# A new decoding of the float64 weights, a new first score step and a new order of issue in an attention and spatial-gate kernel

## The chip, the cores and the metric

The kernel runs on one core of a Trainium2 chip. The metric is the device time of one execution in microseconds (us), from the first to the last instruction of the core with what lies around them; the median of several runs is compared. TensorE (PE) multiplies, VectorE (DVE), ScalarE (ACT) and GpSimd (POOL) work on elements, SyncE (SP) only issues transfers (DMA). Every engine works off its own queue in order and waits at an instruction whose inputs are not there.

## What is computed

Two steps: attention against 32 memory slots for each of 8 batches and 8 heads, and a gated feed-forward over all heads together, whose gate mixes the 576 tokens by a spatial matrix.

```python
def _attn_ref(q, k, v, phi):                 # q, k, v: 8, 8, 576, 64; phi: 8, 8, 576, 32
    a = np.exp(phi - np.max(phi, axis=2, keepdims=True))
    a = a / (np.sum(a, axis=2, keepdims=True) + 1e-09)
    k_m = np.einsum('bhsm,bhsd->bhmd', a, k)
    v_m = np.einsum('bhsm,bhsd->bhmd', a, v)
    scores = np.matmul(q, k_m.transpose(0, 1, 3, 2)) / np.sqrt(q.shape[-1])
    scores = scores - np.max(scores, axis=-1, keepdims=True)
    attn = np.exp(scores)
    attn = attn / (np.sum(attn, axis=-1, keepdims=True) + 1e-09)
    return np.matmul(attn, v_m)

def _moe_ref(x, w_in, w_spatial, b_spatial, w_out):   # x: 8, 576, 512, heads side by side
    h = np.maximum(x @ w_in, 0.0)            # w_in: 512, 1024
    u, v = (h[..., :512], h[..., 512:])
    v_n = (v - mean(v)) / np.sqrt(var(v) + 1e-06)
    v_s = np.einsum('ts,bsd->btd', w_spatial, v_n) + b_spatial[None, :, None]
    return (u * v_s) @ w_out                 # w_out: 512, 512
```

`w_in` and `w_out` arrive as float64. The kernel reads each number as two 32-bit words and makes an fp32 number of them on chip; this is called decoding below.

## The kernel before

The work is cut into steps with one letter each; a function is a generator, and every `yield` ends one step. For each batch b:

- P (`memory_weights`): loads `phi` (single buffer `phi_sb`), takes the maximum over tokens, exponentiates, sums (`es`). The maximum and the sum run over 9 rows of a partition by `over_rows`, in four operations each.
- K (`memories`): loads `k` and `v` (single buffer `kv_sb`), multiplies them by the exponentials (`kvm`, 144 matmuls as the trace counts them), divides by the sums, transposes to `kT` and `vT`.
- Q (`queries`): loads `q` and transposes it to `qT`, for b = 0 on TensorE from one plain load, for b > 0 on VectorE from four loads whose packets are 128 bytes.
- S (`scores`): `sc` = memory slots on partitions, tokens along the row; four VectorE transposes to `sm`, softmax there, transposes back, then the split into a rounded part `ah` and its remainder `al`.
- M0, M1 (`products`): `mp` = `vT` times the decoded `win_sb`, the u half (0) or the v half (1); split into `mh` and `ml`.
- V0 to V4 (`gate`): `pv` = attention times M's v half, for 128 tokens (V4 for 64); relu, mean and variance on VectorE, the inverse root in three small POOL operations, the normalisation on ScalarE, then the split into `vh` and `vl`, `t1` and `t2` for V4.
- U0 to U3 (`units`): `pu`, the u half, relu. G0 to G3 (`spatial`): `ps` = the normalised gate times the transposed spatial matrix `wth`, `wtl`, 28 matmuls; product with `u`; split into `gh`, `gl`. O0 to O4 (`project`): `po`, 12 matmuls, and the store.

Once for the program: D loads `w_in`, L and E decode its u and v half in two blocks of 1024 numbers a partition each, X loads and decodes `w_out` in four blocks of 512, W loads the spatial matrix, T0 to T4 (`transpose_spatial`) transpose it.

Which engine an edit of a step takes is decided by the set `ON_VECTOR`: a remainder (`low`) that is not in it is made on TensorE by one matmul with `minus` and copied out by ScalarE; decoding operations that are not in it go to POOL or ScalarE.

The order is written out by hand. `START` lists the steps of batch 0 with the weight steps, and first steps of batches 1 and 2 (one prime ahead of a batch each); `PLAN` is walked for b = 1 to 7. Inside `manual_schedule` each engine gets its instructions in the order in which the steps issue them. PSUM has four single banks (`bank`) and two double ones (`banks`); a step that finds none free makes TensorE wait for the engine that empties one.

## Time and profile before

| | us |
|---|---|
| median of 3 runs | 422.83 |
| lowest and highest run | 422.32, 423.84 |
| span of the profiled execution | 421.1 |

| engine | busy us | share of the span |
|---|---|---|
| PE | 392.9 | 93% |
| DVE | 295.7 | 70% |
| ACT | 237.0 | 56% |
| POOL | 76.7 | 18% |

The profiled execution is one run; its span ends with the last instruction, and 1.7 us lie between it and the median. A busy PE is one that has a matmul in it, not one at its peak; the matmuls are pipelined, so what counts is the distance between two starts. In the chain that ended last, PE has 83% of the span. The page's 40 slices show PE below nine tenths in the first five (2, 1, 8, 7, 7 tenths of 10.5 us each) and in the last. The DMA engines are busy at nine tenths in the first slices and at about half later.

### The profile page before, as it was taken

The numbers are of one execution on the slowest core, as the hardware profiler recorded it, in microseconds if no ns is written. First come the engines' busy times: TensorE is split into PE (matmuls) and PEld (weight loads), VectorE is DVE, ScalarE is ACT, GpSimd is POOL, SyncE is SP. The second block draws the span as 40 slices with busy tenths as digits, with TensorE's granted clock in tenths as the row PEclk, the third lists the DMA queues.
The fourth block names the chain that finished last, engine by engine and source line by source line (L and its number), as shares of the span: only waits on it lengthen the run. The fifth ranks groups of instructions, "written<-read, shape, count | busy, mean of one in ns | idle before, by whom it ended". The sixth has DMA issues, their size and how long they took to land.

```text
span 421.1 us, 9279 instructions
## 1 busy us (share of the span) xinstructions
PE 392.9 (93%) x3828; PEld 331.0 (79%) x3828; DVE 295.7 (70%) x560; ACT 237.0 (56%) x446; POOL 76.7 (18%) x154
## 2 busy tenths in 40 slices
PE   2187799999999999999999999999999999999995
PEld 1072687979888897979798898879797888889884
DVE  2889998994997568945896569946996568834420
ACT  2948888666743575447735575346735576248321
POOL 1336046522200121022200120002100120013000
PEclk9999999999999999999999999999999999999998
DMA  8999947118922748084905467064905400020003
GB/s 291 399 379 277 199 143 156 12 50 165 196 86 55 128 170 170 2 131 134 227 7 71 111 195 146 1 132 141 198 27 75 107 2 2 2 100 2 0 26 100
DMA packets 85790, 50.69 MB, mean 120 GB/s; under 512 B 66226, under 2 KB 70322, under 8 KB 85748
## 3 DMA queue, kind: packets, MB, share of 16 engines
q1 hardware_dynamic: 85748, 50.10, 47.7%
q8 instruction: 30, 0.49, 0.5%
q14 instruction: 12, 0.10, 0.1%
HBM read 40.65 MB, written 9.44 MB: 119 GB/s over the span
## 4 chain that ended last, share of the span: by engine, by line
PE 83%; DVE 7%; ACT 3%; DMA 3%; issue 2%; POOL 1%; POOLq 0%; SPq 0%; DVEq 0%; ACTq 0%
PE ps L701 28%; PE po L741 23%; PE pu L663 11%; PE pv L597 9%; PE kvm L375 4%; PE mp L565 3%; PE sc L492 2%; DMA w_sb<-in_moe_w_spatial_dram 2%; DMA out_dram<-o 1%; ACT raw L208 1%; PE pv L607 1%; PE pv L606 1%; PE wt L287 1%; DVE phi_sb L349 1%; DVE win_sb L223 1%
## 5 line engine op out<-in xcount | busy, mean ns | idle before, releaser
L701 PE MATMUL ps<-wth,vh 128*128 128x288 f32 x256 | 57.0, 304 | 0.3 <-ACT vh L639 0.3
L723 ACT CAST gh<-g 128x512 fp32r<-128x512 f32 x32 | 19.8, 620 | 63.8 <-DVE g L712 63.6
L701 PE MATMUL ps<-wth,vl 128*128 128x288 f32 x256 | 54.9, 296 | 0.0
L701 PE MATMUL ps<-wtl,vh 128*128 128x288 f32 x256 | 54.5, 294 | 0.0
L626 POOL TENSOR_SCALAR rs<-mv 128x1 f32<-128x1 f32 (+1 forms) x40 | 9.1, 227 | 248.3 <-DVE mv L623 247.9
L741 PE MATMUL po<-woh,gl 128*128 128x512 f32 x128 | 50.8, 397 | 0.0
L741 PE MATMUL po<-woh,gh 128*128 128x512 f32 x128 | 50.5, 395 | 0.0
L701 PEld LDWEIGHTS ps<-wth,vh 128*128 128x128 f32 x256 | 41.1, 188 | 11.5 <-ACT mh L574 5.0
L741 PE MATMUL po<-wol,gh 128*128 128x512 f32 x128 | 50.1, 391 | 0.0
L747 ACT COPY o<-po 128x512 f32<-128x512 f32 x36 | 21.1, 587 | 45.4 <-PE po L741 29.0
L701 PEld LDWEIGHTS ps<-wth,vl 128*128 128x128 f32 x256 | 41.1, 188 | 0.3 <-DVE vl L641 0.3
L701 PEld LDWEIGHTS ps<-wtl,vh 128*128 128x128 f32 x256 | 41.0, 188 | 0.0
L636 ACT ACTIVATE vr<-vr,sh,rs 128x512 f32<-128x512 f32 (+1 forms) x40 | 32.5, 814 | 9.3 <-POOL sh L631 9.0
L621 DVE BATCH_NORM_STATS2 st<-vr 128x6 f32<-128x512 f32 (+1 forms) x40 | 27.5, 687 | 14.0 <-ACT vr L602 13.8
L712 DVE TENSOR_TENSOR g<-u,ps 128x576 f32<-128x576 f32 x32 | 23.4, 751 | 12.5 <-PE ps L701 12.5
L741 PEld LDWEIGHTS po<-woh,gl 128*128 128x128 f32 x128 | 24.0, 188 | 7.5 <-DVE gl L725 2.1
L663 PE MATMUL pu<-ah,mh 128*128 128x288 f32 x128 | 28.8, 306 | 0.4 <-ACT u L672 0.4
L544 DVE TENSOR_TENSOR al<-aT,ah 128x576 fp32r<-128x576 f32 x16 | 12.1, 754 | 23.6 <-ACT ah L542 23.6
L741 PEld LDWEIGHTS po<-wol,gh 128*128 128x128 f32 x128 | 24.1, 188 | 4.6
L741 PEld LDWEIGHTS po<-woh,gh 128*128 128x128 f32 x128 | 24.0, 188 | 4.7
L663 PE MATMUL pu<-al,mh 128*128 128x288 f32 x128 | 27.4, 295 | 0.0
L663 PE MATMUL pu<-ah,ml 128*128 128x288 f32 x128 | 27.3, 294 | 0.0
(158 smaller groups left out, 887.3 us busy)
## 6 DMA issues: line engine op xcount, KB each, us to landing
kv_sb<-in_k_dram SPq DMA_DIRECT2D x8, 1152.0 KB, 7.2
kv_sb<-in_v_dram SPq DMA_DIRECT2D x8, 1152.0 KB, 8.2
out_dram<-o SPq DMA_DIRECT2D x32, 256.0 KB, 2.0
q_sb<-in_q_dram SPq DMA_DIRECT2D x28, 288.0 KB, 6.1
phi_sb<-in_phi_dram SPq DMA_DIRECT2D x8, 576.0 KB, 4.3
raw<-in_moe_w_in_dram SPq DMA_DIRECT2D x8, 512.0 KB, 8.0
raw_out<-in_moe_w_out_dram SPq DMA_DIRECT2D x4, 512.0 KB, 6.0
w_sb<-in_moe_w_spatial_dram SPq DMA_DIRECT2D x1, 1152.0 KB, 6.9
```

Source lines behind the costliest of these rows:

```text
L375: nc.tensor.matmul(kvm[r][32 * j : 32 * j + 32], phi_sb[halves[r], j, i, :], kv_sb[halves[r], j, :, i * D : (i + 1) * D], start=(i == 0), ...
L544: nc.vector.tensor_tensor(al[:, r], aT[:, r], ah[:, r, 0:S].bitcast(F32), op=ALU.subtract)
L565: nc.tensor.matmul(mps[r][32 * j : 32 * j + 32, :], vT[D * r : D * r + D, 32 * j : 32 * j + 32], win_sb[D * r : D * r + D, j, cs], start=True,
L597: nc.tensor.matmul(pv, x[:, r, cs], m[:, r, DM:DFF], start=(n == 0), stop=(n == 5))
L621: nc.vector.bn_stats(st6, vr)
L636: nc.scalar.activation(vr, vr, AF.Identity, bias=sh, scale=rs)
L663: nc.tensor.matmul(pu[:, hf, 0:HALF], m[:, r, cs], a[:, r, hf * HALF : (hf + 1) * HALF], start=(n == 0), stop=(n == 5),)
L701: nc.tensor.matmul(ps[:, hf, 0:HALF], a, w[:, hf * HALF : (hf + 1) * HALF], start=(n == 0), stop=(n == len(ops) - 1),)
L712: nc.vector.tensor_tensor(g.rearrange("p (a s) -> p a s", a=2), u[:, dt, :].rearrange("p (a s) -> p a s", a=2), ps[:, :, 0:HALF], op=ALU.mult,
L723: nc.scalar.copy(hi, x)
L741: nc.tensor.matmul(po, a, w, start=(n == 0), stop=(n == 11))
L747: nc.scalar.copy(o, po)
```

## The change

**Decoding.** A block of 1024 numbers a partition took three to five VectorE operations (exponent, mantissa, sign, and often the sum of mantissa and low word and the product), two or three on ScalarE, and POOL operations where `ON_VECTOR` left them there. Now it takes two on ScalarE (L181 on the low words, L187 on the high words, a scale each) and two on VectorE (L183 and L189). `w_out` is loaded and decoded in two blocks of 1024, in the buffers of `w_in`'s u half; POOL makes its `woh` and `wol`, one operation each per block.

**Phi.** The four operations of `over_rows` become one `tensor_reduce`, always on VectorE, which reads `phi_sb` with the 9 rows innermost, 128 bytes apart.

**First scores.** For b = 0, `scores_first` makes `sc` with tokens on partitions: 72 small matmuls instead of 16 long ones; softmax without VectorE transposes; then nine TensorE transposes, three ScalarE casts `ah` and three VectorE subtractions `al`, both of which write with a stride of 9 numbers.

**Spatial transposes.** One double bank takes all 576 columns, so that a T step has one cast `wth` (or `ws1`) of 576 and one remainder of 576, where there were two each.

**Order of issue.** `START` and `PLAN` are new. Cut to the core of the diff:

```diff
 START = """
-    P*5 W P D1 P T1 W P*2 D1 P D0 P E0 D0 L0 D0 T2 T1 E0 L0 T1 E0 L0 E0 D0 W T1 L1 K T2 L0 L1 T2
+    Q*3 P Q*2 P Q*3 P K Q P*3 K Q D1 P*3 D1*2 K*2 D1 E0 K*3 E1 K P' K*3 Q S E0 S E1 P' E1 S K E0 S W
...
-ON_VECTOR = set(
...
-    E0.add E0.mul L0.add L1.add L1.mul wtl10 wtl1512 wtl40 X0.add X1.add X1.mul X1.wol es1 ml110
-    ml111 ml100 ml101 es2 es3 es5 es6 es7
...
+ON_VECTOR = set("wtl1 wtl4 ml110 ml111 ml100 ml101 E0 E1 L0 L1 X0.sign X1.sign".split())
...
-        nc.vector.tensor_scalar(
-            power, hi, 20, 0x7FF, op0=ALU.logical_shift_right, op1=ALU.bitwise_and
...
+    def decode(tag, w, name):
...
+        nc.scalar.activation(low, low.bitcast(U32), AF.Copy, scale=0.875 * 2.0**-29, bias=0.49)
+        yield
+        engine(name).scalar_tensor_tensor(
+            low, high, -(2**31), low, op0=ALU.bitwise_and, op1=ALU.bitwise_or
         )
         yield
...
+        nc.scalar.activation(f, f, AF.Copy, scale=2.0**-112)
+        yield
+        nc.vector.scalar_tensor_tensor(
+            high if w is None else w.bitcast(I32),
+            high,
+            3,
+            low,
+            op0=ALU.logical_shift_left,
             op1=ALU.bitwise_or,
         )
...
+            nc.gpsimd.tensor_copy(hi, w)
+        yield
+        engine(f"X{n}").tensor_tensor(lo, w, hi.bitcast(F32), op=ALU.subtract)
...
-        half = one.tile([P, NJ, 4, MEM], F32, name="half")
-        eng.tensor_tensor(half, phi_sb[:, :, 0:4], phi_sb[:, :, 4:8], op=op)
...
+    def over_rows(to, op):
+        nc.vector.tensor_reduce(to, phi_sb.rearrange("p j i m -> p j m i"), axis=AX.X, op=op)
         yield
...
+    def scores_first(b):
...
+                        nc.tensor.matmul(
+                            sc[D * r : D * r + D, (i // 2 * NJ + j) * MEM :][:, 0:MEM],
+                            qT[rows, block, D * r : D * r + D],
+                            kT[rows, r, MEM * j : MEM * j + MEM],
...
+        token = lambda x, i: x.rearrange("p r (s i) -> p i r s", i=NX)[:, i]
...
+            x = ta[:, 0 : GI * P].rearrange("p (i r s) -> p i r s", i=GI, r=2)
+            nc.scalar.copy(token(ah[:, :, 0:S], i), x)
...
```

Three places of the new order, engine by engine.

SP, the start of its queue: the loads of the first stretch. `raw` is a piece of a float64 weight (half a block). Before:

```order
L330 DMA phi_sb<-in_phi_dram 128x4x288
L260 DMA w_sb<-in_moe_w_spatial_dram 128x4x576
L261 DMA w_rem<-in_moe_w_spatial_dram 64x576
L263 DMA b_sb<-in_moe_b_spatial_dram 1x576 x2
L178 DMA raw<-in_moe_w_in_dram 128x1024 x6
L363 DMA kv_sb<-in_k_dram 128x4x576
L363 DMA kv_sb<-in_v_dram 128x4x576
L178 DMA raw<-in_moe_w_in_dram 128x1024
L434 DMA q_all<-in_q_dram 128x4x576
L178 DMA raw<-in_moe_w_in_dram 128x1024
```

The same place now:

```order
L172 DMA raw<-in_moe_w_in_dram 128x1024 x4
L284 DMA phi_sb<-in_phi_dram 128x4x288
L233 DMA w_sb<-in_moe_w_spatial_dram 128x4x576
L234 DMA w_rem<-in_moe_w_spatial_dram 64x576
L236 DMA b_sb<-in_moe_b_spatial_dram 1x576 x2
L172 DMA raw<-in_moe_w_in_dram 128x1024 x2
L317 DMA kv_sb<-in_k_dram 128x4x576
L317 DMA kv_sb<-in_v_dram 128x4x576
L172 DMA raw<-in_moe_w_in_dram 128x1024 x2
L172 DMA raw<-in_moe_w_out_dram 128x1024 x2
L284 DMA phi_sb<-in_phi_dram 128x4x288
L414 DMA q_sb<-in_q_dram 32x72x32 x4
```

Ahead of these rows the queue now has `q`, `phi`, `k` and `v` of batch 0. The v half of `w_in` is loaded first; batch 1's `phi`, the spatial matrix, the first block of the u half, batch 1's `k` and `v`, and the second block follow, then `w_out`, batch 2's `phi` and batch 1's `q`.

ACT, the last instructions ahead of the first long run of matmuls. `mp` are the products, `wt` the transposed spatial matrix. Before, ahead of the first U and V:

```order
L574 CAST mh<-mp_1_0_447 128x512
L164 CAST ml<-mp_0_1_415 128x512
L164 CAST ml<-mp_1_0_447 128x512
L542 CAST ah<-aT 128x576
L574 CAST mh<-mp_1_1_448 128x512
L164 CAST wtl<-wt_400 128x64
L164 CAST wtl<-wt_354 128x64
L164 CAST ml<-mp_1_1_448 128x512
```

Now, ahead of the first V; `L181` and `L187` are decoding, `L310` the exponential of batch 1's phi:

```order
L260 CAST ws_93<-wt_399 128x576
L260 CAST wth<-wt_423 128x576
L488 CAST ah<-ta_434 128x3x2x64
L583 CAST mh<-mp_1_1_388 128x512
L488 CAST ah<-ta_445 128x3x2x64
L187 ACTIVATE raw<-raw 128x1024
L310 ACTIVATE phi_sb<-phi_sb 128x1152
L488 CAST ah<-ta_454 128x3x2x64
L181 ACTIVATE raw<-raw 128x1024
L260 CAST wth<-wt_461 128x576
L160 CAST ml<-mp_1_1_388 128x512
```

The cast `ml` of the v half, which the first V reads, is now the 20th of 20 ScalarE instructions that begin with the first cast of the transposed spatial matrix: 7 casts or copies of 576, 5 of 512, 3 `ah`, 3 of 1024 for decoding, an exponential of 1152 and one small copy. M0 moves behind the first three V.

DVE, after the first V steps. Before, batch 1's `q` is transposed (L478) one at a time between other work:

```order
L621 BN_STATS st_717<-vr 128x6
L623 BN_AGGR mv<-st_717 128x2
L251 TENSOR_TENSOR wol<-raw_out,woh 128x512
L478 STREAM_TRANSPOSE qT<-q_sb 128x576
L641 TENSOR_TENSOR vl<-vr,vh 128x512 x2
L210 SCALAR_TENSOR_TENSOR power<-raw_out,power 128x512
L218 SCALAR_TENSOR_TENSOR raw_out<-raw_out 128x512
L478 STREAM_TRANSPOSE qT<-q_sb 128x576
```

Now three of the four stand together (L423), ahead of the last decoding operation of `w_out`'s first block (L189), of `vl` and of the statistics of V3:

```order
L626 TENSOR_TENSOR vr<-vr,pv_4_629 64x512
L630 BN_STATS st_703<-vr 64x6
L632 BN_AGGR mv<-st_703 64x2
L423 STREAM_TRANSPOSE qT<-q_sb 128x576 x3
L189 SCALAR_TENSOR_TENSOR raw<-raw 128x1024
L295 TENSOR_REDUCE cm<-mt_728 128x2
L650 TENSOR_TENSOR vl<-vr,vh 128x512 x2
L423 STREAM_TRANSPOSE qT<-q_sb 128x576
L630 BN_STATS st_825<-vr 128x6
L632 BN_AGGR mv<-st_825 128x2
```

POOL has `woh` and `wol` of that block, 1024 numbers each, ahead of the inverse root of V3. In the repeated part, 24 matmuls of G and a transpose stood between S and the next M on PE; now six matmuls of G stand there. The last steps were O1 and O4, whose store is two transfers; now the last is O2 with one.

## Rows read from the trace of the kernel before

**Rows 1.** Stretches: length, busy us (count) by engine, TensorE clock, DMA, GB/s

```profile
20.00:48.26 28.26, 21.31 (x438) 13.96 (x438) 26.69 (x42) 19.65 (x44) 10.49 (x6) 1.00 1.06 285
48.26:97.00 48.74, 48.26 (x337) 40.44 (x325) 44.20 (x91) 35.63 (x66) 20.50 (x26) 1.00 0.44 118
97.00:386.00 289.00, 288.92 (x2882) 247.65 (x2881) 205.20 (x396) 159.08 (x300) 37.52 (x101) 1.00 0.45 99
386.00:416.60 30.60, 30.21 (x176) 26.46 (x174) 9.48 (x19) 11.13 (x23) 2.48 (x6) 1.00 0.09 35
```

**Rows 2.** Timeline of PE: start, length, instruction, count

```profile
22.90 3.71 PE L375 MATMUL kvm<-kv_sb,phi_sb 64*32 64x128 f32 x144
45.02 2.25 PE L375 MATMUL kvm<-kv_sb,phi_sb 64*32 64x128 f32 x144
48.59 0.43 PE L663 MATMUL pu<-ah,mh 128*128 128x288 f32 x2
50.19 0.39 PE L597 MATMUL pv<-mh,ah 128*128 128x512 f32 x1
50.42 0.39 PE L597 MATMUL pv<-ml,ah 128*128 128x512 f32 x1
```

**Rows 3.** Timeline of DVE, its first instruction and the load that released it

```profile
4.82 0.69 DVE L319 TENSOR_TENSOR half<-phi_sb 128x512 f32<-128x512 f32 x1 [4.82 <-DMA phi_sb<-in_phi_dram]
```

**Rows 4.** DMA in two stretches of the start, by the view of group 1

```profile
4.00:27.00 23.00, 9.96 (x180) 7.47 (x180) 16.11 (x22) 11.30 (x20) 6.81 (x6) 1.00 1.04 392
37.00:47.50 10.50, 7.68 (x176) 3.80 (x168) 10.26 (x14) 7.87 (x16) 4.62 (x3) 1.00 1.17 145
```

**Rows 5.** DVE groups by line and shape: busy, mean ns, idle before

```profile
L210 DVE SCALAR_TENSOR_TENSOR power<-raw,power 128x1024 int32<-128x1024 int32 x4 | 4.7, 1203 | 0.0
L478 DVE STREAM_TRANSPOSE qT<-q_sb 128x576 f32<-128x576 f32 x28 | 20.5, 752 | 6.6 <-DMA q_sb<-in_q_dram 4.0 <-issue 2.7
L538 DVE STREAM_TRANSPOSE aT<-sm 128x288 f32<-128x288 f32 x28 | 11.7, 455 | 0.2
L517 DVE TENSOR_REDUCE rsum<-sm 128x36 f32<-128x1152 f32 x8 | 10.8, 1347 | 0.0
L533 DVE STREAM_TRANSPOSE aT<-sm 128x256 f32<-128x256 f32 x4 | 2.4, 645 | 0.0
```

**Rows 6.** ACT groups by line and shape

```profile
L356 ACT ACTIVATE phi_sb<-phi_sb 128x1152 f32<-128x1152 f32 x8 | 9.4, 1170 | 3.3 <-DVE phi_sb L349 3.3
L574 ACT CAST mh<-mp 128x512 fp32r<-128x512 f32 x32 | 18.6, 583 | 11.7 <-PE mp L565 11.7
L636 ACT ACTIVATE vr<-vr,sh,rs 128x512 f32<-128x512 f32 x32 | 26.0, 813 | 8.4 <-POOL sh L631 8.1
```

**Rows 7.** Timeline of ACT: two instructions back to back

```profile
14.60 1.16 ACT L205 ACTIVATE power<-power,rebias 128x1024 int32<-128x1024 int32 x1
15.66 2.15 ACT L208 ACTIVATE raw<-raw 128x1024 f32<-128x1024 uint32 x2
```

**Rows 8.** POOL groups by line and shape

```profile
L226 POOL TENSOR_TENSOR win_sb<-win_sb,power 128x512 f32<-128x512 f32 x4 | 7.7, 1928 | 7.2 <-DMA raw<-in_moe_w_in_dram 7.2
L251 POOL TENSOR_TENSOR wol<-raw_out,woh 128x512 fp32r<-128x512 f32 x3 | 4.5, 1509 | 0.9 <-ACT woh L249 0.8
L627 POOL TENSOR_TENSOR rs<-rs,half_neg 128x1 f32<-128x1 f32 x32 | 18.5, 579 | 2.7
```

**Rows 9.** Chain that ended last, in order of time: start, length, what

```profile
67.49 1.88 PE mp L565 x32
97.24 1.59 PE pu L663 x12
110.24 1.13 PE sc L492 x32
```

**Rows 10.** Timeline at the end: the last stores

```profile
417.21 0.47 SPq L752 DMA_DIRECT2D out_dram<-o  x1
417.73 0.59 SPq L753 DMA_DIRECT2D out_dram<-o  x1
```

More of the change, by code (lines that the diff above doesn't have):

```diff
@@ L158, in low @@
             n = x.shape[0]
-            tensor.matmul(
-                x, minus[0:n, 0:n], hi, start=False, stop=True, skip_group_check=True
-            )
+            cut = x.shape[1] if x.shape[1] <= 512 else 256
+            for cs in (slice(0, cut), slice(cut, x.shape[1])):
+                if cs.start < cs.stop:
+                    tensor.matmul(
+                        x[:, cs],
+                        minus[0:n, 0:n],
+                        hi[:, cs],
+                        start=False,
+                        stop=True,
+                        skip_group_check=True,
+                    )
         yield
@@ L227, in decode @@
[L227 to L251 removed]
+        state["decoded", tag] = f
@@ new lines, in memory_attention_spatial_gate, with load_win, decode_win, prepare_out @@
+    RAW = ("gh", "gl"), ("vh", "vl")
+    def load_win(b, c):
+        for n in range(2):
+            yield from load(RAW[c][n], w_in, n, slice(c * 512, (c + 1) * 512))
+    def decode_win(b, c, n):
+        yield from decode(
+            RAW[c][n], win_sb[:, 2 * n : 2 * n + 2, c * 512 : (c + 1) * 512], f"{'LE'[c]}{n}"
+        )
+    def prepare_out(b, n):
+        yield from load(RAW[0][n], w_out, n, slice(0, DM))
+        yield from decode(RAW[0][n], None, f"X{n}.sign")
+        w = state["decoded", RAW[0][n]]
+        hi, lo = state["wo", n] = tuple(
+            one.tile([P, 2, DM], F32R, tag=f"{part}{n}", name=part) for part in ("woh", "wol")
+        )
+        if f"X{n}" in ON_VECTOR:
+            nc.scalar.copy(hi, w)
+        else:
+            nc.gpsimd.tensor_copy(hi, w)
+        yield
+        engine(f"X{n}").tensor_tensor(lo, w, hi.bitcast(F32), op=ALU.subtract)
@@ L264, in load_spatial @@
         yield
-        w_dup = one.tile([P, NI, 2, SR], F32, tag="grh", name="w_dup")
-        w_rem_dup = one.tile([SR, 2, SR], F32, tag="grl", name="w_rem_dup")
-        state["dup"] = w_dup, w_rem_dup
-        for c in range(2):
-            nc.scalar.copy(w_dup[:, :, c, :], w_sb[:, :, SM:S])
-            yield
-            nc.scalar.copy(w_rem_dup[:, c, :], w_rem[:, SM:S])
-            yield
     def transpose_spatial(b, si):
         w_sb, w_rem, _ = state["spatial"]
-        w_dup, w_rem_dup = state["dup"] if si == NI else (None, None)
-        tp = banks(f"wt_{si}")
+        tp = banks(f"wt_{si}").rearrange("p a s -> p (a s)")
+        part = tp[:, 256 : 256 + S]
         for ti in range(NI + 1):
@@ L453, in queries @@
                 cs = slice(j * P, (j + 1) * P)
[L454 removed]
                 nc.tensor.transpose(tq[0:D, cs], q_sb[:, j, 8 * D :], ident)
             yield
[L457 to L463 removed]
+            nc.scalar.copy(qT[0:D, 16:20].rearrange("p n s -> p (n s)"), tq[0:D])
+            yield
             return
```

250 lines of the change are left out of this document (109 added, 141 removed).

## The prediction

> **What bounds the kernel now.** I read the stretches first. From 48.3 us to 416.6 us TensorE (PE) has a matmul in it nearly all the time: 288.92 us of the 289 between 97 and 386, 30.21 of the last 30.6 [rows 1]. [...] Between 20 and 48.3 us PE is busy 21.31 of 28.26, VectorE (DVE) 26.69 [rows 1]: here DVE is the bound. What the change can win lies ahead of the first long run of matmuls at 48.59 [rows 2]; what it can lose is any new wait of PE behind it.
>
> **The change part by part.** Five terms; the start first.
>
> *Decoding.* Each block of 1024 keeps two DVE operations of about 1.2 us (as L210 [rows 5]) and two of ScalarE (ACT), 1.06 apart [rows 7]. For `w_in` DVE has 8 operations where it had 17 in the trace, so it stops being the bound. ACT has as many as before, and is not relieved. The question is what comes last instead: the loads or ACT.
>
> *Loads.* At the start the queues move 392 GB/s [rows 4]. The first DVE instruction starts at 4.82 on a `phi` of .59 MB [rows 3]; .59 MB is 1.5 us at that rate, and I split the rest into 2.3 us until bytes flow and 1.0 from the last byte to its use. In the new order q, phi, k, v (4.13 MB) then end at 12.8, the v half of `w_in` (2.10) at 18.2. Batch 1's phi needs the buffer that K of batch 0 reads: K starts at 13.8 and takes 3.7 as the first K did (the second took 2.25, and the clock doesn't tell why [rows 1, 2]), so with about 1.5 for the issue bytes flow from 19.2 to 20.7. The spatial matrix (1.33) ends at 24.1 and is usable at 25.1, the first block of the u half at 26.8, batch 1's k and v (2.36) at 32.8, the second block at 35.5, usable at 36.5.
>
> *ACT.* The first V needs `ml` of the v half, the last of the 20 ACT instructions of the order. With each instruction's mean less the .1 by which neighbours overlap [rows 7], that is 5 of 512 at .48 [rows 6], 7 of 576 at .54 (scaled), 3 `ah` at .5 (estimate, 384 strided numbers), 3 of 1024 at 1.06, the exponential at 1.07 [rows 6] and .2: 12.2 us. The first cast of the spatial matrix can start about 27.2 (25.1 and two transposes of blocks with their copies, an estimate of 2). With .9 of waits for PE the chain ends at 40.3. Two other chains end there too: the exponential of batch 1's phi ends at 37.7 in it, and K of batch 1 (2.3 [rows 2] and .3 of start) stands ahead of that V on PE, hence 40.3; the last block of `w_in`, usable at 36.5, has two DVE and an ACT operation left, which are not needed until M0, about 44.5.
>
> *The lead.* From 40.3 PE has V2, V0, V1 (18 matmuls, 4.2), M0 1.9 [rows 9], V4 .9, two small transposes .3, two remainder matmuls .7, U2 and U3 (24, 3.2) and about .5 of waits: 52.0. Before, the same work without M0 and remainders, which were done already, ran from 48.59 for 4.2 + .9 + .3 + 3.2 to 57.2. The lead is **5.2 us**.
>
> *The new wait: `vh` of V3.* The order of DVE puts three transposes of q and L189 ahead of V3's statistics, and POOL has `woh` and `wol` of 1024 ahead of V3's root. PE goes from 52.0 through M1 of batch 1 (1.9), V3 (1.4), U1, U0 (3.2) and waits of .1 to 58.6, then 36 matmuls of G (4.75) and S (1.13 [rows 9]) to 64.5, where it first needs V3's `vh`. The other side: the `w_out` block takes the buffer of `w_in`'s first u block, free at about 37.8, and lands about 42.0; phi of batch 2 follows until 43.5, then q of batch 1, whose 128-byte packets kept the queues at 145 GB/s for 10.5 us [rows 4]: landed 54.0, usable 55.0. Three transposes at .7 [rows 5] end at 57.1, L189 at 58.2. POOL's two-input work cost 1.5 (L251) to 1.9 (L226) for 512 numbers [rows 8], so `wol` costs 3.0 to 3.9 for 1024; `woh`, one input, has no row, 1.3 at the rate of other engines up to 3.0. That is 62.5 to 65.1; three small POOL operations of .5 (L627 [rows 8]), the normalisation .8 (L636 [rows 6]) and `vh` .6 give 65.4 to 68.0. PE waits .9 to 3.5. From nothing (if POOL waits for neither) to 4.3 (if V4's remainder, behind an ACT scale, is later still); I take **-2.2**, the middle, as both ends rest on the same two rows.
>
> *The repeated part.* Six matmuls of G, .8 us, stand between S and M where 24 and a transpose (3.3) did. M takes banks that DVE empties by its four transposes of `sc`, .46 each as L538 [rows 5], and by then V3's remainders and statistics may be ahead. Two banks are enough to start. Gaps of .1 us for each of 7 batches: **-.7**, between 0 and -1.4; more is a rival below. Phi's maximum and sum change from four operations to one of 1152 numbers, 1.35 as L517 [rows 5]; DVE has 205 of 289 us busy [rows 1], so this costs nothing there while PE's work covers it. If DVE fell behind, it would show as the gap just priced.
>
> *The end.* The last store is one transfer, where two were issued .52 apart [rows 10]: **+.5**, between .2 for O2's other position and .6.
>
> Sum: 5.2 - 2.2 - .7 + .5 = 2.8. The profiled span is 421.1; 418.3 remains, and with 1.7 from span to median **420.0 us**.
>
> [...] Five new accesses are strided: `tensor_reduce` of phi reads numbers 128 bytes apart, `ah` and `al` write 36 bytes apart, the transposes' casts don't. The trace has one pair: L538 transposes 288 numbers in 455 ns, 1.6 ns each, L533, whose result is strided, 256 in 645, 2.5 each [rows 5]. [...]
>
> **The rivals.**
>
> B, *more is won.* POOL's copy is at its fast end, or q lands earlier because its packets no longer compete with weights, and V3's `vh` is there in time; or ACT starts its casts a microsecond earlier. Against it: q's rate of 145 GB/s [rows 4] had nothing to do with the weights' bytes alone. Sum 5.2 to 6 + .5 - .7 - (0 to .9): 415 to 418 us. The chance is .22.
>
> C, *strided accesses eat it.* With L533's ratio of 1.6 [rows 5] a reduction costs 2.2 instead of 1.35. Both stand in the chain of K: .85 for batch 0's maximum, .85 for batch 1's sum, and `ah`, `al` .2 to .3 each on ACT and DVE; with K of batch 1 at 3.7 instead of 2.3 [rows 2], V starts at 43.2. Lead 2.3, the wait at V3 then some 1.5 (its other side doesn't move): 2.3 - 1.5 - .7 + .5 = .6, **422.2 us**. The chance is .18.
>
> D, *slower: M waits for banks of S.* Before, 3.3 us of G covered the four DVE transposes; now .8 does. If DVE's maximum `cm`, a remainder and V3's statistics (.7 each) stand ahead of the transposes in each batch, PE waits for them with nothing else to issue, since its queue is in order: 1.0 us in each of 7 batches instead of .1, -7.0. 5.2 - 2.2 - 7.0 + .5 = -3.5: **426.3 us**. It decides from some .7 us a batch. For it speaks that the order has less cover; against it DVE's share of 71% in the steady part [rows 1], and that the four `sc` banks are emptied one by one. The chance is .20.
>
> That the change doesn't do what it says would show as V starting at 48 us again; then only the end's .5 is left and the waits cost, which C and D cover.
>
> **How the numbers follow.** The forecast's mechanism (lead about 5, V3 waits) has .40, between 418 and 421.5; B .22, C .18, D .20. A measurement of this kernel can tell .3%, 1.3 us, from no change: faster is under 421.5, slower over 424.1. Faster takes A and B, .62; same C, .18; slower D, .20. The range leaves out the far half of D and a little of B: 414.5 to 425.5.
>
> **What would show it.** First V at about 40 (right) or 43 to 48 (wrong, C); ACT without idle time from 27 to its `ml`; the second block of the u half released by its load at 36.5; the exponential of batch 1's phi ending at 37.7. A wait of PE at the first G matmul of V3's `vh` between 64 and 68, released by ACT and behind it by POOL: without it, B. The reduction of phi at 1.35 or 2.2. Gaps ahead of each `mp` in the repeated part: .1 for the forecast, about 1 for D. If PE starts the long run at 40 and the time is not under 421.5, the lead was given back later, and the gaps say where.

## The result and the profile after

The changed kernel takes 429.44 us (median of 4 runs, 427.46 to 430.34); the kernel before took 423.12 beside it. The ratio is 1.0132, interval 1.0095 to 1.0169: slower by 1.3%, where 420.0 was predicted and the range ended at 425.5. The profiled execution is the run of 427.46, with a span of 425.1.

The stretches of the kernel after, by the same view as [rows 1] (length, busy us and count of PE, weight loads, DVE, ACT, POOL, granted clock, DMA share, GB/s):

```profile
20.00:48.26 28.26, 24.30 (x375) 18.38 (x376) 22.75 (x27) 19.66 (x35) 0.94 (x2) 0.70 0.75 259
48.26:97.00 48.74, 45.23 (x319) 36.46 (x318) 42.85 (x62) 30.46 (x53) 17.50 (x20) 1.00 0.55 131
97.00:386.00 289.00, 286.50 (x2864) 247.88 (x2863) 213.81 (x371) 155.67 (x298) 34.86 (x96) 1.00 0.45 101
386.00:421.30 35.30, 35.30 (x213) 31.71 (x212) 12.53 (x24) 14.94 (x28) 3.67 (x9) 1.00 0.09 29
```

VectorE is indeed relieved in the first stretch: 22.75 us busy, where [rows 1] has 26.69. But PE is idle behind 48.26 us for 48.74 - 45.23 + 289.00 - 286.50 = 6.0 us; before, by the same sum up to its last matmul at 416.6, it was 0.95. And the clock of the first stretch is 0.70. Single stretches of it, by the same view (the first K, what stands between it and the first scores, the first scores, the spatial transposes):

```profile
14.30:17.90 3.60, 3.60 (x160) 3.60 (x160) 2.19 (x1) 1.16 (x1) 0.00 (x0) 0.59 1.02 419
17.90:21.20 3.30, 1.09 (x21) 0.48 (x5) 2.38 (x5) 2.51 (x7) 0.00 (x0) 0.92 0.66 198
21.20:28.60 7.40, 7.40 (x145) 7.37 (x144) 5.43 (x5) 3.71 (x6) 0.00 (x0) 0.50 0.95 286
28.60:37.80 9.20, 8.88 (x46) 5.00 (x43) 6.88 (x10) 5.10 (x9) 0.00 (x0) 0.50 1.02 385
```

PE is busy nearly without a break from 21.2 to 37.8 (16.28 of 16.60 us), with the granted clock at 0.50. Single lines of the timeline of PE (start, length, instruction, count, and in brackets the idle time and what ended it), with what stands between them left out, answer to [rows 2]:

```profile
14.28 3.69 PE L329 MATMUL kvm<-kv_sb,phi_sb 64*32 64x128 f32 x144 [2.20 <-ACT phi_sb L310]
21.21 7.50 PE L441 MATMUL sc<-kT,qT_all 64*64 64x32 f32 x144
28.64 1.11 PE L249 MATMUL wt<-ident,w_sb 128*128 128x128 f32 x4
43.90 2.25 PE L329 MATMUL kvm<-kv_sb,phi_sb 64*32 64x128 f32 x144 [1.14 <-ACT phi_sb L310]
47.14 0.50 PE L606 MATMUL pv<-mh,ah 128*128 128x512 f32 x1 [0.49 <-DVE den L351]
68.69 0.53 PE L710 MATMUL ps<-wth,vl 128*128 128x288 f32 x2 [1.77 <-DVE vl L650]
74.23 0.53 PE L710 MATMUL ps<-wth,vh 128*128 128x288 f32 x2 [0.69 <-ACT vh L648]
114.16 0.30 PE L292 MATMUL mt<-ident,mx 128*128 128x128 f32 x1 [1.14 <-DVE mx L279]
282.60 0.23 PE L341 MATMUL kvm<-ones,es 64*32 64x2 f32 x4 [1.37 <-issue]
```

The reader is to see three things. The first scores (72 matmuls in the program, 144 as the trace counts them) take 7.5 us. The first V starts at 47.14, where 40.3 was forecast. And five waits of 0.7 us or more stand behind it: 0.7 at 54.9 (for the `mh` of the u half, not shown above), 1.8 and 0.7 in the first G steps, 1.1 for phi's maximum of batch 2, and 1.4 inside K's last matmuls at 282, which the profile can put down to nothing. The repeated part by itself is as long as before: from the M at 116.8 to the one at 352.2 it takes 235.4 us after, and 235.6 before (114.8 to 350.4). The stop of 1.4 at 282 lies inside it, so without that stop the new order is some 1.6 us shorter there.

The load of the spatial matrix, which the prediction's chain starts from (issue at 18.4, landing 9.0 later, that is at 27.4):

```profile
L233 SPq DMA_DIRECT2D w_sb<-in_moe_w_spatial_dram x1: 1193/1193/1193, 18.4 to 18.4; - x1
DMA to landing us min/median/max: 9.0/9.0/9.0
```

The reduction of phi, by groups (busy us, mean ns, idle before), and VectorE beside POOL around 65 us (the last line is the view of the tile `vl` from 64 to 69 us, with the shortest, median and longest of the two in ns):

```profile
L279 DVE TENSOR_REDUCE es<-phi_sb 128x128 f32<-128x1152 f32 x8 | 18.3, 2285 | 2.2 <-ACT phi_sb L310 2.2
L279 DVE TENSOR_REDUCE mx<-phi_sb 128x128 f32<-128x1152 f32 x8 | 18.0, 2244 | 8.2 <-DMA phi_sb<-in_phi_dram 8.2
```

```profile
64.14 1.10 POOL L222 CAST woh<-raw 128x1024 fp32r<-128x1024 f32 x1 [1.75 <-DVE raw L189]
64.19 4.44 DVE L650 TENSOR_TENSOR vl<-vr,vh 128x512 fp32r<-128x512 f32 x2
65.33 2.75 POOL L224 TENSOR_TENSOR wol<-raw,woh 128x1024 fp32r<-128x1024 f32 x1
L650 DVE TENSOR_TENSOR vl<-vr,vh x2: 1612/2260/2908, 64.2 to 65.7; 128x512 fp32r<-128x512 f32 x2
```

The reduction takes 2.24 to 2.29 us, not the 1.35 of an unstrided one [rows 5]. Two `vl`, some 0.7 us each elsewhere, take 4.44 together. The first takes 1.61 and ends 0.6 us behind the end of POOL's copy `woh`; the second takes 2.91 and ends 0.6 behind the end of `wol`.

### The profile page after: what moved, and what is told of

Its sections match the earlier page's. It is cut to its first block, busy times and chain, and to the rows that moved or that the text cites. A ratio compares the mean times of both kernels' runs of the same rounds, so it can differ in the third digit from the quotient of the medians.

```text
span 425.1 us, 9400 instructions
## 1 busy us (share of the span) xinstructions
PE 400.5 (94%) x3949; PEld 342.3 (81%) x3949; DVE 299.6 (70%) x489; ACT 229.3 (54%) x423; POOL 58.8 (14%) x136
## 4 chain that ended last, share of the span: by engine, by line
PE 80%; DVE 8%; ACT 6%; DMA 2%; POOL 1%; issue 1%; SPq 0%; POOLq 0%; ACTq 0%; DVEq 0%
PE ps L710 27%; PE po L750 21%; PE pu L672 9%; PE pv L606 8%; PE mp L574 3%; PE kvm L329 3%; PE sc L441 2%; PE sc L508 2%; DMA phi_sb<-in_phi_dram 2%; DVE vl L650 1%; PE wt L249 1%; ACT vr L645 1%; DVE es L279 1%; DVE mx L279 1%; POOL rs L636 1%
## 5 line engine op out<-in xcount | busy, mean ns | idle before, releaser
L635 POOL TENSOR_SCALAR rs<-mv 128x1 f32<-128x1 f32 (+1 forms) x40 | 10.2, 256 | 276.9 <-DVE grl L734 173.8
L650 DVE TENSOR_TENSOR vl<-vr,vh 128x512 fp32r<-128x512 f32 x32 | 25.0, 784 | 21.6 <-ACT vh L648 21.6
L611 ACT ACTIVATE vr<-pv 128x512 f32<-128x512 f32 x32 | 19.3, 602 | 23.3 <-PE pv L606 23.2
L672 PE MATMUL pu<-ah,ml 128*128 128x288 f32 x128 | 27.4, 296 | 0.1
L672 PE MATMUL pu<-al,mh 128*128 128x288 f32 x128 | 27.4, 296 | 0.0
```

The source lines that it names most:

```text
L611: nc.scalar.activation(vr, pv, AF.Relu)
L650: nc.vector.tensor_tensor(vl[:, st, :], vr, vh[:, st, :].bitcast(F32), op=ALU.subtract)
L672: nc.tensor.matmul(pu[:, hf, 0:HALF], m[:, r, cs], a[:, r, hf * HALF : (hf + 1) * HALF], start=(n == 0), stop=(n == 5),)
```

## The experiments

All changes are made to the kernel after, or to the kernel before where the text says so. The changed kernel's own runs span 2.9 us, so a difference under 2 between the medians of two such kernels rests on the traces, not on the times. Where a text below says how much earlier the last matmul ends, it compares the two profiled executions; in the changed kernel it ends at 421.3.

### The two-input operation on POOL

```diff
-ON_VECTOR = set("... X0.sign X1.sign".split())
+ON_VECTOR = set("... X0.sign X1.sign X0 X1".split())
```

> The changed kernel with woh on ScalarE and wol on VectorE instead of both on POOL. Theory: in the changed kernel VectorE's second vl stood still from about 65 to 68.1 us because POOL's wol ran from 65.33 to 68.08 on the same operands' memory; without it vl takes 0.7, PE's waits of 1.8 us (for vl) and 0.7 (for vh) at V2 and V3 go, although VectorE gets 1.3 more for each block: 1.5 to 2.5 us less. Rival: the wait is VectorE's own queue (three transposes of q and a decoding operation); then the wait stays or grows by the 1.3, and the time is the same or 1 us more.

427.24 us, 2.2 less. The timeline of VectorE at the same place, and PE's first G matmul:

```profile
64.78 0.68 DVE L650 TENSOR_TENSOR vl<-vr,vh 128x512 fp32r<-128x512 f32 x1
66.37 0.69 DVE L650 TENSOR_TENSOR vl<-vr,vh 128x512 fp32r<-128x512 f32 x1 [0.92 <-ACT vh L648]
66.98 1.22 DVE L224 TENSOR_TENSOR wol<-raw,woh 128x1024 fp32r<-128x1024 f32 x1
66.94 0.54 PE L710 MATMUL ps<-wth,vh 128*128 128x288 f32 x2 [1.20 <-ACT u L681]
```

`vl` takes 0.7 each, `wol` 1.2 on VectorE where POOL took 2.75, and the 36 matmuls of the first G steps take 5.0 us from start to end instead of 7.2. The theory holds for the wait, and POOL's copy takes part: both of its operations stopped a subtraction of VectorE's, 4.44 us for 1.4 us of work. By what means is not shown. Not every operation is stopped: beside the second block's `wol` (77.77 to 80.20 in the changed kernel) two VectorE transposes and a reduction took their usual 0.44 to 0.48 and 1.35 us.

What is won is smaller than the wait. `woh` stands on ScalarE now, ahead of the `u` that the first G needs, and PE waits 1.2 us for it; in the five later kernels that take this edit over (e8, e13, e15 to e17) it waits 1.3 to 2.6 there. The last matmul ends 0.4 us earlier than in the changed kernel, so no trace shows the rest of the 2.2.

### The strided reduction

```diff
     def over_rows(to, op):
-        nc.vector.tensor_reduce(to, phi_sb.rearrange("p j i m -> p j m i"), axis=AX.X, op=op)
+        half = one.tile([P, NJ, 4, MEM], F32, name="half")
+        nc.vector.tensor_tensor(half, phi_sb[:, :, 0:4], phi_sb[:, :, 4:8], op=op)
...
```

> The changed kernel with the maximum and sum of phi in four contiguous VectorE operations (together 1.64 us in the trace of before) instead of one strided reduction (2.24). If both reductions stand in the chain that sets the first V, that V starts 1 us earlier and the time falls by about 1, and the wait of 1.1 us for the maximum at 112.7 shrinks to 0.5. If other work covers them, nothing changes.

426.28 us, 3.2 less (425.83 to 429.68 over 7 runs). The wait ahead of `mt` at 113 shrinks from 1.1 to 0.2 us, and batch 1's K starts at 42.80 instead of 43.90. But this K takes 3.53 us, with the granted clock at 0.50 up to 45.5; the first V starts at 46.29, 0.85 earlier, and the last matmul ends 1.2 earlier. That is about what was expected; the rest of the 3.2 no trace shows. The other way round, into the kernel before:

```diff
-        half = one.tile([P, NJ, 4, MEM], F32, name="half")
-        eng.tensor_tensor(half, phi_sb[:, :, 0:4], phi_sb[:, :, 4:8], op=op)
...
+        nc.vector.tensor_reduce(to, phi_sb.rearrange("p j i m -> p j m i"), axis=AX.X, op=op)
```

> The kernel before with the single strided reduction (2.24 us) for phi's maximum and sum, always on VectorE, instead of four operations (1.64 on VectorE, some on POOL). Theory: three of these stand in the full VectorE stretch before 50 us, so the first V comes 1 to 1.5 us later, and the time rises by as much; in the repeated part it is hidden. Rival: fewer instructions make up for the stride, and nothing changes.

431.43 us against 423.33: 8.1 more, where 1 to 1.5 were expected. The start gives 2.1 (first U at 50.71 instead of 48.59 [rows 2]); the rest lies behind it, most of it in the repeated part, which "is hidden" got wrong. One batch, VectorE and then PE:

```profile
205.96 2.29 DVE L317 TENSOR_REDUCE mx<-phi_sb 128x128 f32<-128x1152 f32 x1
208.17 0.68 DVE L616 BATCH_NORM_STATS2 st<-vr 64x6 f32<-64x512 f32 x1
...
209.05 0.74 DVE L473 STREAM_TRANSPOSE qT<-q_sb 128x576 f32<-128x576 f32 x1
```

```profile
208.81 0.71 PE L487 MATMUL sc<-qT,kT 64*32 64x288 f32 x12
209.84 1.16 PE L487 MATMUL sc<-qT,kT 64*32 64x288 f32 x20 [0.32 <-DVE qT L473]
```

The same place of the kernel before, on VectorE:

```profile
200.07 0.68 DVE L319 TENSOR_TENSOR half<-phi_sb 128x512 f32<-128x512 f32 x1
...
201.55 0.73 DVE L478 STREAM_TRANSPOSE qT<-q_sb 128x576 f32<-128x576 f32 x1
```

There the order lets the four short operations be parted by others: only the first stands ahead of the last transpose of q. One long operation stands ahead of it in a piece, and S waits: from start to end it takes 2.2 us here instead of 1.2. In three batches it is 2.1 to 2.2, in three others 1.5 to 1.6. Whether it is the stride or the work that POOL no longer does (the sums of batches 0 and 4) was told apart by moving those two sums alone:

```diff
-    ml111 ml100 ml101 es2 es3 es5 es6 es7
+    ml111 ml100 ml101 es0 es4 es2 es3 es5 es6 es7
```

> The kernel before with the sums of phi of batches 0 and 4 on VectorE instead of POOL, in the four contiguous operations as before. It tells apart the two things that the single strided reduction did there (8.1 us more): theory: the stride, 0.6 us for each of 16, is nearly all of it, since VectorE is late for the transposes of q that the scores wait for, and this kernel takes 0 to 2 us more than the one before. Rival: it is the work taken from POOL; then 4 us or more.

423.66 against 423.43: nothing. So the single strided reduction costs the old order 8 us, with 16 reductions that are 0.6 us longer each; the new order, in which S stands elsewhere, 1.2 by the traces and 3 by the medians. Whether a contiguous operation in one piece would cost less, no run tells.

### Decoding alone

The new decoding in the kernel before, in the places of the old operations:

```diff
-        nc.vector.tensor_scalar(
-            power, hi, 20, 0x7FF, op0=ALU.logical_shift_right, op1=ALU.bitwise_and
-        )
...
+        nc.scalar.activation(low, low.bitcast(U32), AF.Copy, scale=0.875 * 2.0**-29, bias=0.49)
...
+        nc.scalar.activation(f, f, AF.Copy, scale=2.0**-112)
...
```

> The kernel before with the new decoding alone: each block has two ScalarE and two VectorE operations, in the places of the old ones; order, loads, first scores and phi as before. Theory: VectorE was the bound between 20 and 48 us (26.69 of 28.26 busy), and 9 of its 17 operations on w_in go, some 7 us of work; the first V (50.2) starts 2 to 4 us earlier and the time falls by 2 to 4. Rival: the loads and ScalarE end at the same time as VectorE did, and nothing is won; the time is within 0.5.

424.76 against 423.33, ratio 1.0025 (1.0006 to 1.0043): the rival. PE waits twice for ScalarE's `mh` (1.6 us, not shown, and 1.3), and then batch 1's K runs at half speed:

```profile
43.97 0.79 PE L159 MATMUL mp<-mh,minus 128*128 128x512 f32 x1 [1.26 <-ACT mh L551]
44.56 0.47 PE L159 MATMUL wt<-wth,minus 128*128 128x64 f32 x2
44.96 4.09 PE L352 MATMUL kvm<-kv_sb,phi_sb 64*32 64x128 f32 x144
```

K starts at 44.96, as before (45.02 [rows 2]), but takes 4.09 instead of 2.25, with the granted clock at 0.50. That K is 1.8 us longer, and the first U starts 1.05 later (49.64 for 48.59). All ten runs of this kernel have a mean granted clock of 0.987 to 0.994; the four of the kernel before at 0.987 to 0.992 beside it took 424.9 to 425.2. So the 1.4 can be that clock, and nothing here is won by the new decoding itself: VectorE was full and yet not what set the end. The next attempt took ScalarE's and PE's remainders away:

```diff
-    ml111 ml100 ml101 es2 es3 es5 es6 es7
+    ml111 ml100 ml101 ml010 ml011 ml000 ml001 es2 es3 es5 es6 es7
```

> The kernel before with the new decoding, and the remainders ml of batch 0 on VectorE instead of PE and ScalarE. With the decoding alone PE waited 1.6 and 1.3 us for ScalarE's mh ahead of the remainder matmuls, and the clock fell to 0.50 in the K behind it (4.09 us instead of 2.25). Theory: VectorE has room now and the remainders were what kept the decoding's gain from the first U; without them the run of matmuls starts 1 to 2 us earlier, the clock stays up, and the time falls 2 to 3 us below that with the decoding alone, 1 to 2 below the kernel before. Rival: ScalarE's decoding scales set mh, and the time is that of the decoding alone.

428.60: worse by 3.8 than the decoding alone. K now waits 4.3 us for VectorE's `ml` (its banks), and 135 of its matmuls then take 3.54 us, where all 144 take 2.25 at 1.00. That attempt failed; the remainders were on the better engines.

### The start: first scores, ScalarE's order, the clock

Extra matmuls where PE was idle:

```diff
-    Q*3 P Q*2 P Q*3 P K Q P*3 K Q D1 P*3 D1*2 K*2 D1 E0 K*3 E1 K P' K*3 Q S
+    Q*3 P Q*2 P Q*3 P K Q P*3 K Q D1 P*3 D1*2 Z K*2 Z D1 E0 K*3 E1 K P' K Z K*2 Q S
```

> The changed kernel with 16 extra matmuls of 128 columns (result unread) on PE where it stood idle at the start: 8 ahead of the first K, 4 behind it, 4 between two transposes. Theory 1: the lead was lost to the clock. The granted clock read 0.50 from 13.9 to 17.3 us and from 20.7 to 37.8, and in that stretch the first K took 3.6 us, the 144 small matmuls of the first scores 7.4 and the spatial transposes twice their usual time. If PE's idleness before them lowers the clock, it should now read 1.00 longer, the first scores should take some 3.8 us, the first V should start near 43 instead of 47.1, and the time should fall by 3 to 4 us. Rival: the clock falls all the same, because what runs there is small matmuls; then the first scores stay at 7.4 and the time stays within 1 us. Second rival: the first scores get shorter and the first V still starts at 47, because VectorE and ScalarE are last.

429.57 us. The stretches of the first K, behind it, and of the first scores:

```profile
14.00:17.00 3.00, 2.74 (x162) 2.46 (x163) 2.42 (x3) 0.73 (x2) 0.00 (x0) 1.00 1.03 421
17.00:22.80 5.80, 2.27 (x18) 1.92 (x17) 2.69 (x6) 3.28 (x8) 0.00 (x0) 1.00 1.03 374
23.20:30.60 7.40, 7.40 (x146) 7.33 (x145) 4.54 (x4) 3.15 (x5) 0.00 (x0) 0.50 1.04 360
```

The first K now runs at 1.00 and takes 2.25 instead of 3.69. That won nothing, since the values behind it waited on ScalarE, behind a decoding scale (L181 at 20.46) that waited 2.4 us for its load. The clock fell to 0.50 all the same, and the first scores took 7.5 us as before: so far the first rival. Its reason, that small matmuls lower the clock, isn't shown: the fall stands at 22.8, ahead of the first of them (23.16), and from 18.4 to 21.8 PE had stood idle, for all the extra matmuls; K, 144 small matmuls too, kept 1.00. The first scores started 1.95 us later than in the changed kernel, and the first V 2.0 later (49.16), so here what delayed them delayed everything. Does making them shorter help? First with the old form:

```diff
-        if b == 0:
-            yield from scores_first(b)
-            return
```

> The changed kernel with batch 0's queries and first scores as before: 16 long matmuls and VectorE transposes instead of 144 small matmuls and PE transposes. Theory: PE's 7.4 us of first scores set when the spatial transposes start (28.6); with 2 us instead they start when the spatial matrix is there, about 26, and the first V starts near 44: 2 to 3 us less. Rival: the VectorE work of the old form (some 12 us in a row) becomes the bound, and the first V starts at 47 or later: 0 to 3 us more.

431.33: the rival. The scores take 3.4 and the transposes start at 25.88, 2.8 earlier; but PE then waits 2.8 us for `mh`, VectorE is busy 20.2 of the 22 us from 24 to 46, K takes 4.09, as in e5 at a clock of 0.50, and the first V starts at 50.80, 3.7 later; K's length explains 1.8 of them. The new form is the better of the two here, small matmuls or not. So they were shortened with nothing in their place:

```diff
-        for c, sc in enumerate(scs):
+        for c, sc in enumerate(scs[:1]):
             for i in range(c, NX, 2):
```

> The changed kernel without 64 of the 144 small matmuls of the first scores (those of the odd rows; the even rows' scores are used in their place, so this leaves out part of the computation). Nothing else differs. Theory: these matmuls, .052 us each at the lower clock, stand in the chain to the first V one for one until the spatial matrix is there: the first scores take 4.2 instead of 7.5, the spatial transposes start at about 25.8 instead of 28.6, the first V at 44 to 44.5 instead of 47.1, and the time falls by 2.5 to 3. Rival: ScalarE's order and VectorE's sum of phi stand beside it, and the first V starts at 46 or later: 1 us or less.

431.06, and no answer: the edit itself held a double bank, and the second transpose waited 2.0 us for it. Mended:

```diff
-        for c, sc in enumerate(scs):
-            n = 5 - c
-            x = sc.rearrange("p (i j m) -> p i j m", j=NJ, m=MEM)
+        for c in range(2):
+            n = 5 - c
+            x = sm[:, 0:8:2] if c else scs[0].rearrange("p (i j m) -> p i j m", j=NJ, m=MEM)
```

> The run without 64 of the 144 small matmuls of the first scores again, mended: in the other one the second softmax half read the first half's double PSUM bank, so that bank was held until 29.7 us and the second spatial transpose waited 2.0 us for it. Here the second half reads the first half's numbers from SBUF (part of the computation is left out as before). Theory: the first scores' time on PE stands in the chain to the first V: transposes start at about 26, the first V at 44 to 45 instead of 47.1, 2 to 3 us less. Rival: the chain through VectorE and ScalarE ends at 46 or later whatever PE does; 1 us less at most.

428.58 (427.02 to 431.39). PE's timeline:

```profile
21.68 4.48 PE L441 MATMUL sc<-kT,qT_all 64*64 64x32 f32 x80
26.49 1.11 PE L249 MATMUL wt<-ident,w_sb 128*128 128x128 f32 x4 [0.33 <-DMA w_sb<-in_moe_w_spatial_dram]
...
41.80 3.86 PE L329 MATMUL kvm<-kv_sb,phi_sb 64*32 64x128 f32 x144 [1.17 <-ACT phi_sb L310]
```

The theory holds as far as K: the transposes start 2.15 earlier, the exponential of batch 1's phi is earlier by as much, and K starts 2.1 earlier. But not all of this is the scores' work: the transposes now wait for the spatial matrix, which lands at 26.4 here and at 27.4 in the changed kernel, so 1.0 of the 2.15 came with the load. Then K takes 3.86 instead of 2.25 (clock 0.50 from 42.0 to 45.4), and the first V starts at 46.06, 1.1 earlier. Half of the gain went to the clock. Behind it PE stops longer than in the changed kernel (2.7 us at 101, see below; the clock stands at 0.50 from 103.5 to 110.3 behind that), and the profiled execution, the slowest of the four, is 3.9 longer than the changed kernel's. The other candidate, ScalarE's order:

```diff
-    K*3 E1 K P' K*3 Q S E0
+    K*4 P' K*3 E1 Q S E0
...
-    S D0 S L0 S L0 S X0 M1 T1 P' S T3 P' S X0 L1 T1 K' S K' M1 B T3
+    S D0 S S S M1 P' S P' S K' S K' M1 L0*2 X0*2 T1 T3 L1 T1 B T3
```

> The changed kernel with two moves in ScalarE's order: the casts and decoding scales that the first V doesn't need (two of the u half's decoding, one cast of the spatial matrix) stand behind the remainder ml that it needs, and the first decoding scale stands behind the first K's copies. Theory: after the first scores ScalarE's order is the last thing (it is full from 38.3 to 46.6); three instructions of 1.2, 1.2 and 0.7 less in front of ml, and the first scores 1 us earlier: the first V starts 2 to 3 us earlier (44 to 45), the time falls by 1.5 to 3. Rival: the first V waits for VectorE's sum of phi and for K of batch 1, which stand beside it; then it gains 1 us or less, or M0 waits for what was moved back and nothing is won.

429.19: the rival. The first scores start 0.9 earlier, but the transposes then wait 1.1 us for the spatial matrix, which lands at 28.4. The exponential starts at 41.59 instead of 42.68 and K 1.05 earlier, but the first V only 0.5 (46.61), and the decoding that was moved back comes up as waits: 3.3 us for `vl` instead of 1.8.

### The causes together, and batch 1's K

e2 and e3 in one kernel:

> The changed kernel with two of its parts taken back together: woh on ScalarE and wol on VectorE (alone it measured 2.2 us less), and phi's maximum and sum in four contiguous operations (alone 3.2 less). If the two waits are apart, the gains add up: 424 us, the time of the kernel before. If the second only moved what the first then waits for, 425 to 426.

427.41: the gains don't add up. The waits of 1.8 and 1.1 are gone or halved, but PE waits 1.3 for `u`, S waits 1.0 for `kT`, and the mean granted clock of the profiled run is 0.964, where the changed kernel's has 0.974.

```diff
-    S D0 T4 S M1 S D0 S L0 S L0 S X0 M1 T1 P' S T3 P' S X0 L1 T1 K' S K' M1 B T3 K'*3
+    S D0 T4 P' S M1 S D0 S S M1 S P' S S K' S K' M1 L0*2 X0*2 L1 T1 B K'*3
```

> The changed kernel with all the named causes taken back or eased at once: woh and wol off POOL, phi's maximum and sum in four contiguous operations, the exponential of batch 1's phi and the remainder ml ahead of decoding scales and casts that the first V doesn't need, one spatial transpose behind the first V, the first decoding scale behind the first K's copies. Theory: the exponential ends near 41.7 instead of 43.8, K of batch 1 runs 2 us earlier, the first V starts at 44.5 to 45.5, no wait for vl of 1.8 us follows: 423 to 425, level with the kernel before; and without the strided reductions and POOL's wol nothing of the changed kernel is left that costs. Rival: the start's engines are all near full, and what is moved back comes up as a wait at M0, at vh or at vl: 426 or more.

429.07: the rival, and the theory that the named causes make up the loss falls in this form. The exponential starts 4.1 us earlier (38.62), yet the first V at 46.49: PE waits 2.5 us for the second `mh`, which now stands behind that exponential on ScalarE, and 135 of K's matmuls take 3.60 us. Behind it PE waits 2.2 for `u`. A step taken ahead puts another behind. This trace also shows what the clock does to the first scores, since it falls within them:

```profile
20.30:21.20 0.90, 0.90 (x32) 0.90 (x32) 0.00 (x0) 0.90 (x2) 0.00 (x0) 1.00 1.07 387
21.30:22.20 0.90, 0.90 (x23) 0.90 (x21) 0.88 (x1) 0.45 (x1) 0.00 (x0) 0.50 0.89 343
```

Two of these matmuls start every 0.059 us in the first stretch and every 0.107 in the second. So all 144 at 1.00 would take about 4.2 us instead of 7.5 (an estimate, 72 times 0.059). What could still be tried was the clock at batch 1's K:

```diff
+        if b == 1:
+            for _ in range(4):
+                nc.tensor.matmul(kvb[0][:, 256:384], ident, ident, start=True, stop=True)
         for i in range(NX):
```

> The changed kernel with woh and wol off POOL, phi's maximum and sum in four contiguous operations, and four matmuls of 128 columns on PE ahead of batch 1's K, where PE waits for the exponential anyway. Where the start was shortened, that K fell to the lower clock (3.5 to 4.1 us instead of 2.25) and kept half of the gain. Theory: PE at work ahead of it keeps the clock at 1.00, K takes 2.25, the first V starts at 45.5 to 46, 425 to 426 us. Rival: the clock falls at 43 all the same: 427.4 as with the two parts alone.

```profile
41.49 1.05 PE L333 MATMUL kvm<-ident 128*128 128x128 f32 x8
42.79 2.25 PE L337 MATMUL kvm<-kv_sb,phi_sb 64*32 64x128 f32 x144 [0.25 <-ACT phi_sb L315]
...
45.56 0.50 PE L614 MATMUL pv<-mh,ah 128*128 128x512 f32 x1 [0.49 <-ACT ml L160]
...
66.42 0.85 PE L718 MATMUL ps<-wth,vh 128*128 128x288 f32 x2 [2.59 <-ACT u L689]
```

K takes 2.25 and the first V starts at 45.56, the earliest of the kernels here: as expected. The median is 426.59, but over 10 runs from 423.79 to 430.05. The best of them is level with the kernel before; the median is not. The last matmul ends at 420.7, only 0.6 earlier than in the changed kernel, though V starts 1.6 earlier: behind it PE waits 0.9 us for `mh`, 2.6 for `u`, 0.9 for phi's maximum, 1.0 for `kT`, and 0.8 in a stop without a releaser.

### Stops without a releaser

```diff
+                for _ in range(60 if j == 0 else 0):
+                    nc.tensor.matmul(tq[0:32, 0:2], ident[:, 0:32], ident[:, 0:2], start=True, stop=True)
```

> The changed kernel with 60 tiny matmuls (32 by 32, two columns, result unread) on PE ahead of the first transposes of q, where PE waits 6 us for the load anyway. In the changed kernel's trace PE stops 1.4 us inside K's burst of small matmuls at 281 us, released by nothing that the profile shows; six kernels with the same number of PE instructions ahead stop in the same burst, two with 64 fewer stop at 101, 191 and 330, one with 28 more at 143 instead. Theory: the stop belongs to PE's supply of instructions and goes by the count of instructions ahead; here it leaves 281 and stands in another burst or none, and the rest of the trace is as in the changed kernel: 1.5 us less to 3 more. Rival: it belongs to that batch's transfers; then it stays at 281.

430.90: the extra matmuls were not free (they pushed the start back by about 2 us). But the stop is not at 281 any more. The kernel with 60 more matmuls, inside a K:

```profile
235.93 2.15 PE L329 MATMUL kvm<-kv_sb,phi_sb 64*32 64x128 f32 x132
238.84 0.33 PE L329 MATMUL kvm<-kv_sb,phi_sb 64*32 64x128 f32 x6 [0.75 <-issue]
```

Then the kernel of e15 with 24 and with 120 of these matmuls:

> As e15, with 24 tiny matmuls ahead of everything on PE. By the theory of e14 only the stops inside K's bursts move; the time differs from e15 by what they weigh, up to 3 us either way.

> As e15, with 120 tiny matmuls ahead of everything on PE. As e16: the stops inside K's bursts move, or vanish.

428.77 and 434.69. In e16 the stops stand at 47 (1.1 us), 105 (0.8, inside a U), 188 (1.5) and 328 (0.4); in e17 there is one at 239 (0.5). The first V starts 2.9 and 9.1 us later than in e15, so these kernels tell of the stops' places and not of what they cost. The place of a stop goes with the count of PE instructions ahead of it. The changed kernel, e2, e3, e7, e8, e13 and e15 (which has eight matmuls more ahead) stop behind the 2893rd or 2894th matmul of the trace, at 280 to 285 us. e9 and e12, with 64 fewer, stop behind the 982nd (2.7 to 2.8 us at 101 to 103), the 1873rd (0.6 to 0.7 at 191) and the 3275th (0.8 to 1.1 at 330). e1 has one at 143 (0.7), e4 one inside an O at 145 (0.6) and one at 287 (0.7). No trace of the old order (five kernels) has one over 0.5 us. That it is the supply of instructions fits, but no view shows it; that part stays open.

## Why the prediction was wrong

The 9.4 us between 420.0 and 429.44 go to these steps.

**The lead: 5.2 forecast, about 0.3 measured.** The long run starts at 47.14, 1.45 ahead of 48.59, but has 1.1 us more matmuls left (368.1 us of busy time to the end against 367.1). The step that failed is the chain that puts the first V at 40.3, and in it four terms.

- The load: the spatial matrix was to be usable at 25.1, at 392 GB/s; it landed at 27.4. The queues moved 198 GB/s from 17.9 to 21.2 and 286 from 21.2 to 28.6. In the other traces of the new order in which PE waited for the matrix it came between 25.9 and 28.4.
- The first scores: the sum did not have them. The chain took PE as free when the matrix landed, and their 144 matmuls kept it until 28.6, 1.2 us longer; e12, with 64 fewer, starts the transposes as the matrix lands.
- The clock: [rows 1] has 1.00 in every stretch, but the trace of before holds no granted clock ahead of 25.9 us, and the first K there took 3.71 against 2.25 later; the prediction noted the ratio, priced the first K at 3.7 and took no clock term elsewhere. After, that K has 0.59 with 3.69, the scores and the transposes 0.50. By the estimate above the scores alone would have been done 3 us earlier at 1.00, before the matrix landed; four transposes take 1.11 us from 28.64 and 0.60 from 38.07, at 1.00.
- The sum of phi, at 1.35 instead of 2.29. This is the rival C's price, worked out at 2.2 by the ratio of L533 [rows 5]: it was in the text, with .18 and on the wrong side of the choice.

The first V is 6.8 us late. Of this 3.5 stand ahead of the transposes (28.64 for 25.1), 2.6 between them and the end of the exponential (43.85 for 37.7), and 0.7 behind. ScalarE, named as the chain, was full only from 38.3 on, since it waited for PE until then; there the forecast's 20 instructions did set the exponential. What each term alone would give back is not shown: e7, e12 and e13 start the first V 0.5 to 1.1 us earlier and lose all of it behind, e15 1.6 earlier and loses 1.0; only e3 keeps its gain.

**The wait in the first G steps: 2.2 forecast, 2.5 measured (1.8 and 0.7).** The size was right, the mechanism not: V3's `vh` was to be late through the order and POOL's length, by 0.9 to 3.5; it was late by 0.7. The 1.8 are another wait: what came last was `vl` on VectorE, held by POOL's `woh` and `wol` (e2). The price of POOL's operation was in [rows 8]; that it stops another engine was not in the sum.

**The repeated part: 0.7 forecast.** Neither the forecast's gaps of .1 ahead of M nor rival D (banks of S) came: each M of the repeated part follows the matmul ahead of it without idle time, as before. But "this costs nothing there while PE's work covers it", of the reduction, was wrong at 113 (1.1), and the stop at 282 (1.4) was in no view of before. With the small waits PE's idle time behind 48.26 is 5.1 above before's, where the two terms of waits (2.2 and .7) gave 2.9: 2.2 more.

**The end: +.5 forecast.** The span ends 3.8 us after the last matmul instead of 4.6, but the run is 2.4 longer than the span where before it was 1.7 to 1.8: about 0.2 gained, 0.3 less than forecast.

**Span to median.** The profiled run was the fastest; the other three have spans of 426.3 to 428.0, and the median is 2.0 above it. That it was the fastest is luck, and the 2.0 are in no trace. The mean granted clock of the other three is 0.964 to 0.971 against 0.974, so the clock can be a part of it; whether the stops differ too stays open.

Together 4.9 + 2.2 + .3 + 2.0 = 9.4. Rival B had nothing of it; its range was also wrong by its own terms, which give 417.0 to 418.7 and not 415 to 418. C's price of the reduction was right and its account too small: taking the reduction back (e3) brings the first V 0.85 earlier and the end 1.2, and batch 1's K, which C had at 3.7, took 2.25.

**The decoding** did what it says (VectorE 26.69 to 22.75 in the first stretch), and e5 shows that it is worth nothing alone: DVE as "the bound" of the start was the first wrong reading, since a full engine was not the last one.

## What to carry to other kernels

A busy share of 94% in a stretch does not make an engine the bound of what ends it: take the work off it in the old order first (e5) before building a new order on it. Price every instruction of a new form on the engine that runs it, at the clock that stretch has, and look from when on the trace has a clock at all. An engine that is busy 205 of 289 us can still be late: 16 reductions, 0.6 us longer each and no longer parted by other work, cost 8.1 us in the old order (e6). And when work moves to another engine, ask what it now stands ahead of there: `woh` on ScalarE ended one wait of PE (1.8 us for `vl`) and made another (1.2 for `u`, e2).
